# The last output tile of a gated two-branch mixer, divided at column 448 in place of 384

## The chip, the cores and the metric

The kernel runs on one core of a Trainium2 chip. The time is device time in microseconds (us). All runs quoted here are "fast" (an undisturbed clock; the profiles have a granted TensorE clock of 0.998 or 1.0). A profile is one execution; its span is about 1.7 us shorter than the time of the same run (204.5 against 206.2 for the kernel before).

Names used: PE is TensorE, PEld its weight loads, DVE is VectorE, ACT is ScalarE, SP is SyncE, which here only issues DMAs; a trailing q (ACTq, SPq) marks the issue of a DMA by that engine. L515 is line 515 of the kernel. PSUM is the memory in which PE's sums build up, in banks; SBUF is the on-chip memory from which DMAs store. To evict a tile is to copy it from PSUM to SBUF. A store is issued when an engine starts it, and has landed when the last of its 16 completion records has come. Its semaphore is the counter on which SP waits for that.

## The reference, cut to what matters

```python
x = A_x                                            # (1, 2048, 512)
g = _sigmoid((x * gate_w).sum(-1, keepdims=True))
a = _A_ref(x, A_wqkv, A_w_phi, A_wo)               # linear attention, ends in  o @ wo
b = _B_ref(x, B_w_in, B_w_sp, B_b_sp, B_w_out)     # gMLP, ends in (z1 * g) @ w_out
return g * a + (1 - g) * b
```

The output is made in 16 tiles of 128 rows and 512 columns. For each tile, PE accumulates both final products (attention with 4 matmuls, gMLP with 5 matmuls and a remainder) in one PSUM bank. Another engine multiplies the sum by `1 - g` (the gate's other factor is already inside) on its way to SBUF as bf16, and a DMA stores it.

## The kernel before: the parts that matter

Only the last of the 16 tiles is treated specially. Tiles 12, 13 and 14 wait for their remainder matmuls and are stored whole. Tile 15 is computed in two column pieces in two PSUM banks, so that the first piece can be evicted and stored while PE still works on the second.

```python
def ba_attn(acc, tt, start, stop, c0=0, c1=D):
    for g in range(NG):                                      # L509: 4 matmuls
        nc.tensor.matmul(acc, lhsT=oTs[tt][:, g, :], rhs=wo_t[:, g, c0:c1], ...)

def ba_spat(acc, tt, start, c0=0, c1=D):
    i = tt % 2
    for ft in range(5):                                      # L515: 5 matmuls
        nc.tensor.matmul(acc, lhsT=uTs[tt][:, i + ft, :], rhs=w_main[i][:, ft, c0:c1], ...)

def ba_store(acc, tt, c0=0, c1=D, on_dve=False, on_sp=False):
    ob = work.tile([P, c1 - c0], BF16, name=f"ob{c1 - c0}", bufs=4 if c1 - c0 == D else 1)
    dst = out2[tt * P:(tt + 1) * P, c0:c1]
    if on_dve:
        nc.vector.tensor_scalar(                             # L527
            out=ob[:, :], in0=acc, scalar1=g_inv[:, tt:tt + 1], scalar2=None, op0=ALU.mult)
        nc.sync.dma_start(out=dst, in_=ob[:, :])             # L529
    else:
        nc.scalar.activation(out=ob[:, :], in_=acc, func=AF.Copy, scale=g_inv[:, tt:tt + 1])  # L531
        (nc.sync if on_sp else nc.scalar).dma_start(out=dst, in_=ob[:, :])                    # L532

def ba_last():
    last = NT - 1
    ba_step(last - 1)
    pieces = [(acc_tile()[:, 0:384], 0, 384), (bank_tile(q_bank)[:, 0:P], 384, D)]
    for t in BA_GROUPS[-1][:-1]:
        ba_rem(accs[t][:, :], t)                             # L520, remainders of tiles 12 to 14
    for acc, c0, c1 in pieces:
        ba_rem(acc, last, True, c0, c1)                      # L520, remainder of each piece
    for n, t in enumerate(BA_GROUPS[-1][:-1]):
        ba_store(accs[t][:, :], t, on_dve=n == 1, on_sp=True)
    for n, (acc, c0, c1) in enumerate(pieces):
        ba_spat(acc, last, False, c0, c1)
        ba_attn(acc, last, False, True, c0, c1)
        ba_store(acc, last, c0, c1, on_dve=n == 1)           # piece 1: ACT and ACTq; piece 2: DVE and SPq
```

The softmax here doesn't subtract the row's maximum and nothing guards it: scores larger than these inputs give would overflow.

## Time and profile before

| | before |
|---|---|
| time, median of the first 3 runs | 206.33 us (206.13 to 206.88) |
| span of the profiled run | 204.5 us |
| PE busy | 200.8 us, 98% |
| last PE work ends | about 201.7 us |

The first part of the page of the kernel before (engine, busy us, share, instructions) says that PE is busy for almost all of the span:

```profile
PE 200.8 (98%) x1557; PEld 119.9 (59%) x1557; DVE 130.4 (64%) x283; ACT 74.8 (37%) x122; POOL 45.6 (22%) x76
```

The change acts only in the last 5.5 us. This is the end of the chain of waits of the kernel before (start us, us, what):

```profile
199.07 0.54 PE mm L520 x4
199.61 0.92 PE mm L515 x5
200.53 0.65 PE mm L509 x4
201.18 0.28 PE mm L515 x5
201.46 0.24 PE mm L509 x4
201.69 0.02 issue
201.72 0.35 DVE ob L527
```

The second and third lines are the nine matmuls of the 384-column piece; the fourth and fifth are those of the 128-column piece. The chain is followed back from the DVE eviction of the narrow piece: that is the eviction that ended last. The chain stops there and does not show which store landed last; that has to be read from the stores themselves. The timeline of the same stretch shows the two sides that run next to each other (start us, us, engine, line, operation, tile, shapes):

```profile
201.08 0.40 SPq L532 DMA_DIRECT2D out_dram<-ob  x1
201.21 0.58 ACT L531 ACTIVATE ob<-mm,g_inv 128x384 bf16<-128x384 f32 x1 [0.52 <-PE mm L509]
201.29 0.39 PE L509 MATMUL mm<-wspT,oT 128*128 128x128 bf16 x4
201.72 0.35 DVE L527 TENSOR_SCALAR ob<-mm,g_inv 128x128 bf16<-128x128 f32 x1 [1.45 <-PE mm L509]
201.82 0.34 ACTq L532 DMA_DIRECT2D out_dram<-ob  x1
202.09 0.33 SPq L529 DMA_DIRECT2D out_dram<-ob  x1
```

The DMA view of that stretch gives, for each of those two stores, size and us from issue to landing:

```profile
out_dram<-ob ACTq DMA_DIRECT2D x1, 96.0 KB, 1.7
out_dram<-ob SPq DMA_DIRECT2D x1, 32.0 KB, 1.6
```

So the wide piece lands near 201.82 + 1.7 = 203.5 and the narrow one near 202.09 + 1.6 = 203.7.

### The profile page before, as it was taken

Reading aid. Unit: us, or ns where it says so; the run is one execution under the profiler, and the core shown is the slowest. Engines: PE = TensorE matmul, PEld = TensorE weight load, DVE = VectorE, ACT = ScalarE, POOL = GpSimd, SP = SyncE. Lnnn points to the kernel's source line nnn. Section 1 sums busy time; section 2 is a strip of 40 time slices with the busy share of each in tenths; the row PEclk is TensorE's granted clock in tenths of the full one; section 3 lists DMA queues with packets and bytes.
Section 4 is the critical chain, followed back from the end, with each engine's and each line's share of the span. In section 5 each row is a group of like instructions: output and inputs, shape, how many; then the busy total and the mean of one; then the engine's idle time right before and its main releaser. Section 6 shows DMA issues by size and latency. Waiting matters only on the chain.

```text
span 204.5 us, 3996 instructions
## 1 busy us (share of the span) xinstructions
PE 200.8 (98%) x1557; PEld 119.9 (59%) x1557; DVE 130.4 (64%) x283; ACT 74.8 (37%) x122; POOL 45.6 (22%) x76
## 2 busy tenths in 40 slices
PE   8999999999999999999999999999999999999994
PEld 4666666655665555656565666555555555665642
DVE  4567484837977587979797789555566645633332
ACT  3566678796222333332424042222251136002303
POOL 3020202021523325334242442222204220200000
PEclk9999999999999999999999999999999999999999
DMA  6999699999999027940423219853567458552833
GB/s 194 252 205 171 80 151 290 146 278 247 256 249 213 3 38 182 287 94 16 75 48 45 51 38 120 154 109 64 105 161 80 90 113 183 63 96 51 156 64 104
DMA packets 89931, 27.22 MB, mean 133 GB/s; under 512 B 84184, under 2 KB 89912, under 8 KB 89912
## 3 DMA queue, kind: packets, MB, share of 16 engines
q1 hardware_dynamic: 87744, 24.99, 65.4%
q10 hardware_dynamic: 2168, 1.98, 3.5%
q8 instruction: 12, 0.20, 0.4%
q14 instruction: 7, 0.06, 0.1%
HBM read 4.15 MB, written 2.10 MB: 31 GB/s over the span
## 4 chain that ended last, share of the span: by engine, by line
PE 98%; DVE 0%; issue 0%
PE mm L454 37%; PE zp L191 18%; PE mm L355 14%; PE mm L515 9%; PE mm L509 7%; PE mm L395 7%; PE kvacc L411 2%; PE at L467 2%; PE zp L222 1%; PE mm L520 1%; PE zp L307 0%; PE pq L280 0%; PE at L478 0%; PE pq L307 0%; DVE ob L527 0%; PE zp L230 0%
## 5 line engine op out<-in xcount | busy, mean ns | idle before, releaser
L454 PE MATMUL mm<-z2all,wspT 128*128 128x344 bf16 x512 | 79.9, 309 | 0.0
L454 PEld LDWEIGHTS <-wspT 128*128 128x128 bf16 x512 | 49.0, 98 | 25.3
L191 PE MATMUL zp<-w_z,xT 128*128 128x344 bf16 (+1 forms) x254 | 38.1, 310 | 0.0
L359 ACT ACTIVATE eq<-mm 128x512 bf16<-128x512 f32 x32 | 17.4, 594 | 51.4 <-PE mm L355 25.7
L363 DVE TENSOR_REDUCE zs<-eq 128x64 f32<-128x1024 bf16 x16 | 19.5, 1220 | 20.0 <-ACT eq L359 20.0
L191 PEld LDWEIGHTS <-xT 128*128 128x128 bf16 x254 | 24.4, 98 | 11.8
L359 ACT ACTIVATE ek<-mm 128x512 bf16<-128x512 f32 x32 | 17.3, 600 | 27.1 <-PE mm L355 27.1
L459 DVE SCALAR_TENSOR_TENSOR ucat<-mm,bT,z1all 128x344 bf16<-128x344 f32 x32 | 17.4, 544 | 15.0 <-PE mm L454 15.0
L372 POOL TENSOR_TENSOR eq<-eq,ratio 128x512 bf16<-128x512 bf16 x16 | 16.9, 1055 | 44.6 <-DVE ratio L371 36.7
L531 ACT ACTIVATE ob<-mm,g_inv 128x512 bf16<-128x512 f32 (+1 forms) x15 | 10.1, 680 | 33.1 <-PE mm L520 28.5
L363 DVE TENSOR_REDUCE zs<-ek 128x64 f32<-128x1024 bf16 x16 | 19.3, 1209 | 2.8 <-ACT ek L359 2.8
L515 PE MATMUL mm<-wspT,uT 128*128 128x512 bf16 (+2 forms) x85 | 20.1, 367 | 0.0
L355 PEld LDWEIGHTS <-xT 128*128 128x128 bf16 x128 | 12.2, 98 | 12.0
L372 POOL TENSOR_TENSOR ek<-ek,ratio 128x512 bf16<-128x512 bf16 x16 | 16.9, 1056 | 2.2 <-DVE ratio L371 1.7
L509 PE MATMUL mm<-wspT,oT 128*128 128x512 bf16 (+2 forms) x68 | 16.6, 366 | 0.0
L355 PE MATMUL mm<-wq_p,xT 128*128 128x512 bf16 x64 | 16.4, 379 | 0.0
L395 PE MATMUL mm<-wv_sb,xT 128*128 128x512 bf16 x64 | 16.4, 379 | 0.0
L355 PE MATMUL mm<-wk_p,xT 128*128 128x512 bf16 x64 | 16.3, 379 | 0.0
L209 DVE BATCH_NORM_STATS2 bn<-z2all 128x6 f32<-128x344 bf16 x32 | 14.9, 501 | 0.0
L206 ACT ACTIVATE z2all<-zp 128x688 bf16<-128x688 f32 x16 | 11.8, 744 | 7.3 <-PE zp L191 7.2
L260 ACT ACTIVATE z1all<-zp 128x688 bf16<-128x688 f32 x16 | 11.9, 744 | 5.1 <-PE zp L191 4.6
L515 PEld LDWEIGHTS <-uT 128*128 128x128 bf16 x85 | 8.1, 98 | 9.4 <-issue 0.2
(77 smaller groups left out, 142.7 us busy)
## 6 DMA issues: line engine op xcount, KB each, us to landing
out_dram<-ob ACTq DMA_DIRECT2D x12, 128.0 KB, 2.4
wspT<-in_B_w_out_dram SPq DMA_DIRECT2D x2, 640.0 KB, 4.9
w_z<-in_B_w_in_dram SPq DMA_DIRECT2D x2, 344.0 KB, 4.7
w_z<-in_B_w_in_dram SPq DMA_DIRECT2D x3, 172.0 KB, 3.5
wv_sb<-in_A_wqkv_dram SPq DMA_DIRECT2D x2, 256.0 KB, 2.7
wspT<-in_A_wo_dram SPq DMA_DIRECT2D x2, 256.0 KB, 4.0
out_dram<-ob SPq DMA_DIRECT2D x3, 128.0 KB, 1.8
uT<-ucat SPq DMA_TRANSPOSE x16, 2.8
```

The source lines that it names most:

```text
L191: nc.tensor.matmul(zp[:, j, 0:n], lhsT=xT[:, dt, tt * P:(tt + 1) * P], rhs=wt[:, dt, j * HF:j * HF + n], start=(dt == 0), stop=(dt == NDT ...
L209: nc.vector.bn_stats(out=bn6[:, tt, j, :], in_=z2v[:, j, :])
L260: nc.scalar.activation(out=z1all[:, tt, :].rearrange("p (j n) -> p j n", j=2), in_=zp[:, :, 0:HF], func=AF.Gelu_apprx_tanh,)
L355: nc.tensor.matmul(ps[:, :], lhsT=xT[:, dt, tt * P:(tt + 1) * P], rhs=w[:, dt, :], start=(dt == 0), stop=(dt == NDT - 1))
L359: nc.scalar.activation(out=e[:, :, a, :], in_=ps[:, :].rearrange("p (h f) -> p h f", f=DH), func=AF.Exp, scale=1.0 - 2.0 * a)
L363: nc.vector.tensor_reduce(out=z[:].rearrange("p h a -> p (h a)"), in_=e[:].rearrange("p h a f -> p (h a) f"), axis=AX.X, op=ALU.add,)
L372: nc.gpsimd.tensor_tensor(out=e[:, :, 1, :], in0=e[:, :, 1, :], in1=ratio[:, :, None].to_broadcast([P, H, DH]), op=ALU.mult)
L395: nc.tensor.matmul(v_ps[:, :], lhsT=xT[:, dt, tt * P:(tt + 1) * P], rhs=wv_sb[:, dt, :], start=(dt == 0), stop=(dt == NDT - 1))
L454: nc.tensor.matmul(gp[:, 0:HF], lhsT=wspT[:, st, tt * P:(tt + 1) * P], rhs=z2all[:, st, j * HF:(j + 1) * HF], start=(st == 0), stop=(st == ...
L459: nc.vector.scalar_tensor_tensor(out=ucat[tt % NU][:, c0 + j * HF:c0 + (j + 1) * HF], in0=gp[:, 0:HF], scalar=bT[:, tt:tt + 1], in1=z1all[ ...
L509: nc.tensor.matmul(acc, lhsT=oTs[tt][:, g, :], rhs=wo_t[:, g, c0:c1], start=start and g == 0, stop=stop and g == NG - 1)
L515: nc.tensor.matmul(acc, lhsT=uTs[tt][:, i + ft, :], rhs=w_main[i][:, ft, c0:c1], start=start and ft == 0, stop=False)
```

## The change

Its intent is to make the second piece, the one that is evicted and stored after PE's last matmul, smaller, so that less work stands after the end of PE. 64 columns move from the second piece to the first.

```diff
     def ba_last():
         last = NT - 1
         ba_step(last - 1)
-        pieces = [(acc_tile()[:, 0:384], 0, 384), (bank_tile(q_bank)[:, 0:P], 384, D)]
+        cut = D - 64
+        pieces = [(acc_tile()[:, 0:cut], 0, cut), (bank_tile(q_bank)[:, 0:D - cut], cut, D)]
```

## The prediction

> **What bounds the kernel now.** PE is busy 200.8 of the 204.5 us span (98%, the page's first part), and the chain of waits is PE from start to end. The change touches only the last tile, after about 199 us. There the chain ends with five matmuls of L515 and four of L509 on 384 columns (199.61 to 201.18), the same nine on 128 columns (201.18 to 201.69), then the 128-column VectorE eviction (201.72, 0.35 us). The timeline puts the 384-column ScalarE eviction at 201.21 (0.58 us), its output DMA (ACT queue) at 201.82, and the 128-column DMA (SP queue) at 202.09. The DMA view gives 1.7 and 1.6 us to landing: about 203.5 and 203.7. The remaining 0.8 us to 204.5 is SP's closing wait and the end of the program. So two tails run side by side, and the small piece's lands last, by about 0.16 us.
>
> **What the change moves.** No arithmetic, no instruction and no byte is added or removed; 64 columns go from the second piece to the first.
>
> - First piece on PE: in the chain nine matmuls of 384 columns take 1.57 us, 0.174 each at first and 0.1625 in the steady part (0.65 us for four). 512 columns take 0.216 (1.08 us for five), so 448 should take 0.189: nine times 0.027 is +0.24 us.
> - Second piece on PE: 128 columns take 0.056 each (0.28 us for five). The matmuls of 68 columns at L467 take 0.032 each (0.26 us for eight), so 64 columns should take about 0.031, and the weight load is no floor at 0.056. Nine times 0.025 is -0.22 us. The Trainium skill ("TensorE: Matmul & The Clock Gate", Back-to-back issue gap) has N/2.4 + 2.5 ns, and about 60 cycles (25 ns) below 64 columns; the trace's 56 and 216 ns agree with the first. The last matmul thus ends about where it did, +0.00 to +0.03.
> - ScalarE eviction: 0.687 us at 512 and 0.581 at 384, so 0.634 at 448: +0.05.
> - VectorE eviction: 0.751 at 512 and 0.351 at 128, so 0.284 at 64: -0.07.
> - DMA: the first piece grows from 96 to 112 KB, perhaps +0.04 us (an estimate from about 260 GB/s in the windows of 201 to 202.5). The second shrinks from 32 to 16 KB, with as many packets of half the size: little.
>
> **What lies on the critical path.** The first piece's DMA is issued at 201.82 + 0.24 + 0.05 = 202.11 and lands near 203.84. The second's is issued at about 202.04 and lands near 203.60. The end changes hands: the wide ScalarE piece, not the narrow VectorE piece, lands last, about 0.18 us later than the end now. The two DMAs also start within 0.1 us of each other instead of 0.27 and share the engines, which may cost up to 0.2 us more. I predict 206.33 + 0.2 = 206.5 us: slightly slower, below what the 2% test sees. Range 206.15 to 207.0; the before runs alone span 206.13 to 206.88. Faster by over 2%: 0.01; within 2%: 0.98; slower: 0.01.
>
> **What the profile should show.** Everything up to 199 us unchanged; 448-column matmuls 0.189 apart; 64-column ones 0.031 apart; last PE work ending within 0.05 us of 201.69; ScalarE eviction 0.63 us, starting near 201.45; ACT-queue issue near 202.11, after the SP-queue one near 202.04; span about 204.7.
>
> **What would make it wrong.** 64-column matmuls held at the 0.056 us of the 128-column ones (+0.2 us on the second piece); the two nearly simultaneous DMA issues delaying each other; DMA rows of 128 B landing slower than those of 256 B; or a run-to-run shift larger than the effect.

## The result, and the profile after

| | before | after |
|---|---|---|
| time, median of 6 runs each | 206.31 us (205.96 to 206.88) | 206.77 us (206.37 to 207.22) |
| ratio | | 1.002, 95% interval 0.9998 to 1.0043 |
| span of the profiled run | 204.5 us | 204.7 us |

A ratio here is the mean time of one kernel's fast runs over that of the other's fast runs of the same rounds, so it is not quite the ratio of the medians. The interval includes 1: by the timed runs alone, the change could be nothing. The predicted time was 206.5 us; the measured median lies inside the predicted range, but so does 206.31, the time of no change at all. The time alone therefore does not confirm the prediction.

The traces are sharper. Here is the end of the chain of waits of the changed kernel:

```profile
199.07 0.54 PE mm L520 x4
199.61 1.05 PE mm L515 x5
200.66 0.77 PE mm L509 x4
201.43 0.02 issue
201.45 0.63 ACT ob L531
```

The chain now ends in the ACT eviction of the wide piece; the narrow piece is gone from it. In both kernels the last remainders start at 199.07 and the wide piece's matmuls at 199.61. Those took 0.92 + 0.65 = 1.57 us and take 1.05 + 0.77 = 1.82: +0.25 from these rounded figures, +0.24 costed. The timeline:

```profile
201.25 0.31 PE L515 MATMUL mm<-wspT,uT 128*128 128x64 bf16 x5
201.40 0.28 PE L509 MATMUL mm<-wspT,oT 128*128 128x64 bf16 x4
201.45 0.63 ACT L531 ACTIVATE ob<-mm,g_inv 128x448 bf16<-128x448 f32 x1 [0.77 <-PE mm L509]
201.72 0.28 DVE L527 TENSOR_SCALAR ob<-mm,g_inv 128x64 bf16<-128x64 f32 x1 [1.45 <-PE mm L509]
202.03 0.33 SPq L529 DMA_DIRECT2D out_dram<-ob  x1
202.12 0.35 ACTq L532 DMA_DIRECT2D out_dram<-ob  x1
```

The DVE eviction of the second piece starts at 201.72 in both kernels: PE ends at the same moment, because the work on it is only moved. That eviction is 0.07 us shorter and its store is issued 0.07 us earlier (0.06 from the rounded figures shown). The wide piece pays for it: eviction 0.24 us later and 0.05 us longer, store issued at 202.12 in place of 201.82. The DMA view:

```profile
out_dram<-ob ACTq DMA_DIRECT2D x1, 112.0 KB, 1.7
out_dram<-ob SPq DMA_DIRECT2D x1, 16.0 KB, 1.4
```

The wide piece now lands near 203.8 and the narrow one near 203.4. The end of the program has changed hands.

**A cleaner measure.** The start of the first L520 matmul of this last group is a good mark: nothing that the change touches comes before it. I call the time from that mark to the end of the span the *tail*, and the time before it the *head*. Landing times within the tail are the last completion record of each DMA in the trace. The tail is 204.495 - 199.000 = 5.495 us before and 204.735 - 198.999 = 5.736 us after: +0.24 us. Each tail here is that of one profiled execution; the kernel before has only one.

### The profile page after: what moved, and what is told of

Read it like the earlier page. It is cut to its first block, busy times and chain, and to the rows that moved or that the text cites. A ratio compares the mean times of both kernels' runs of the same rounds, so it can differ in the third digit from the quotient of the medians.

```text
span 204.7 us, 3996 instructions
## 1 busy us (share of the span) xinstructions
PE 200.8 (98%) x1557; PEld 119.9 (59%) x1557; DVE 130.3 (64%) x283; ACT 74.7 (36%) x122; POOL 45.6 (22%) x76
## 4 chain that ended last, share of the span: by engine, by line
PE 98%; ACT 0%; issue 0%
PE mm L454 37%; PE zp L191 18%; PE mm L355 14%; PE mm L515 8%; PE mm L395 7%; PE mm L509 7%; PE kvacc L411 2%; PE at L467 2%; PE zp L222 1%; PE mm L520 1%; PE zp L307 0%; PE pq L280 0%; ACT ob L531 0%; PE at L478 0%; PE zp L230 0%; PE pq L307 0%
```

## The experiments

Theory ("race of two tails"): the end is the later of two sides, the wide piece (PE, ACT, ACTq's DMA) and the narrow one (PE, DVE, SPq's DMA). Moving columns shifts one side against the other, and the sum of PE's work does not change. Rivals: the 1.002 is noise; the narrow DMA rows of 128 B are what costs; the two stores issued within 0.09 us of each other delay each other.

All times in this table are us after the mark. Every experiment gave a correct result.

| run | piece 1 (ACT): issued, landed | last piece (DVE): issued, landed | tail | head |
|---|---|---|---|---|
| before, cut at 384 | 2.82, 4.48 | 3.10, **4.65** | 5.50 | 199.00 |
| after, cut at 448 | 3.12, **4.83** | 3.03, 4.45 | 5.74 | 199.00 |
| `cut448_again` | 3.12, **4.82** | 3.03, 4.46 | 5.71 | 199.14 |
| `cut256b` | 2.24, 4.09 | 3.23, **4.82** | 5.65 | 199.52 |
| `cut400` | 2.90, 4.59 | 3.08, **4.79** | 5.64 | 199.28 |
| `cut416` | 2.97, 4.72 | 3.06, **4.89** | 5.74 | 199.96 |
| `cut480` | 3.26, **4.96** | 3.07, 4.74 | 5.79 | 199.03 |
| `dve2_448` | 3.12, 4.83 | 3.35, **5.05** | 5.87 | 199.61 |
| `dve2_384` | 2.83, 4.46 | 3.48, **5.29** | 6.14 | 199.39 |
| `act2_448` | 3.78, **5.47** | 3.03, 4.44 | 6.30 | 198.97 |

The landing in bold is the one that comes last. The head varies by 1.0 us between these profiles (198.97 to 199.96), four times the effect of the change; the tails of the two executions of the same changed kernel differ by 0.02. A span from a single profile, as my early expectations used it, is therefore the wrong measure, and below I read the tails.

### The change again

No edit; the changed kernel timed in five more rounds.

> The changed kernel, unedited, timed again in five rounds. Theory (race of two tails): the wide first piece's ScalarE eviction and DMA end last, 0.24 us later in the span than the narrow piece did before; ratio about 1.001, profile span 204.7. Rival (run-to-run noise made the 1.002): ratio 1.000, and the start of the closing matmuls at L520, not the tail after it, differs between runs.

Measured: 206.69 us median against 206.52 before, ratio 1.0014 (0.9996 to 1.0032). Its tail is 5.712 us (5.736 the first time), its head 0.14 us longer. The timed runs again lean to slower without excluding 1. The rival is half right: most of the scatter between profiles is in the head, yet the tail's +0.22 to +0.24 us repeats. It is 0.11 to 0.12% of the time, within both intervals.

### Other cuts: 400, 416, 480

```diff
-        cut = D - 64
+        cut = 400          # cut416: 416; cut480: 480
```

> Cut at column 400. Race theory: both tails land nearly together, wide piece near 203.60, narrow near 203.65, span 204.5, as before; no gain above 0.02 us. Rival (any narrower second piece costs, through narrow DMA rows of 224 B): span 204.55 or more.

> Cut at column 480. Race theory: the wide piece lands 0.15 us later than at 448 (nine matmuls of 32 more columns +0.12, eviction +0.03), span 204.9, and 32-column matmuls are 0.025 us apart or more. Rival (two DMAs issued within 0.1 us of each other delay one another; here they are 0.25 us apart again): span 204.7 or less.

> Cut at column 416. Race theory: the wide piece is issued 2.97 us after the first closing matmul of L520 and lands at 4.64, the narrow one is issued at 3.06 and lands between 4.55 and 4.75; tail from that matmul to the end of the span 5.48 to 5.60, where the kernel before has 5.495 and the changed one 5.736. Rival (the 400 cut was slow, 5.638, only because its rows of 800 and 224 B begin and end off a 64 B step; 832 and 192 B do not): 5.45 or less.

Measured: cut400 206.21 us against 206.52, ratio 0.9996 (0.9977 to 1.0014); cut416 206.62 against 206.15, ratio 1.0022 (1.0002 to 1.0042); cut480 206.79 against 206.52, ratio 1.002 (0.9998 to 1.0042). The tails are 5.64, 5.74 and 5.79.

cut480 follows the theory. The wide piece lands 0.13 us later than at 448 (0.15 expected), and the rival is out for that piece: the two issues are 0.19 us apart and its store took 1.69 us, against 1.71 at 448. One assumption of the theory fails here: PE ends 0.07 us later (2.75 us after the mark in place of 2.68), since the 32-column matmuls are 0.025 us apart and the 64-column ones 0.029, which saves less than the wider ones cost. The tail grew by only 0.05 us; the section on the closing waits says why.

cut400 and cut416 were misses. The issues fell where I had put them (2.90 and 3.08; 2.97 and 3.06), and the wide piece landed as expected at 400 (1.69 us after issue) and 0.08 us late at 416. But the narrow piece took 1.72 and 1.83 us from issue to landing, where it took 1.55 in the kernel before. cut400's tail is what its rival said (a narrower second piece costs); but at 448 the second piece is narrower still, its rows are 128 B, and it landed after 1.43 us. The timeline of cut416, and below it its DMA view:

```profile
202.93 0.37 ACTq L532 DMA_DIRECT2D out_dram<-ob  x1
203.03 0.33 SPq L529 DMA_DIRECT2D out_dram<-ob  x1
```

```profile
out_dram<-ob ACTq DMA_DIRECT2D x1, 104.0 KB, 1.8
out_dram<-ob SPq DMA_DIRECT2D x1, 24.0 KB, 1.8
```

The two stores are issued 0.09 us apart, ACT's first, and both take 1.8 us. With the same distance and SP's first (the changed kernel) the narrow store takes 1.4. The two differ in width too (96 and 64 columns), so the comparison at one width counts for more: the same 64-column store took 1.43 us issued before ACT's (after) and 1.70 issued 0.23 us behind it (dve2_448, below). The packet records say where it begins: from SP's issue to its first data packet are 0.83 us when SP's is first (after), 0.99 when it follows ACT's by 0.09 (cut416), 0.96 by 0.18 (cut400), 0.96 by 0.23 (dve2_448), 0.86 by 0.27 (before), and 0.83 when ACT's issue is 0.66 us old (dve2_384). That is 0.17 of the 0.40 us between after and cut416; the rest comes behind the first packet, about half of it while the data moves, in part beside the packets of ACT's store, and half between the last data packet and the landing. All 16 reports of the store come late in cut416 (the first 1.65 us after issue, against 1.25), so it is not the single late share that is described further down. So the prediction's warning about nearly simultaneous issues was right for the order ACT, SP and wrong for the order SP, ACT, which is the one that the change produced. The rival about rows off a 64 B step falls: cut416 is on that step and is not faster than cut400. I can show the dependence on order and distance, not what in the DMA path makes it; a cut at 416 with SP's store issued first was not run.

### Cut at 256, and a mistake of mine

```diff
-        cut = D - 64
+        cut = 256
```

> Cut at column 256. Race theory: the second piece, now 256 columns, ends last: its VectorE eviction takes 0.485 us in place of 0.351 and its DMA grows, span 204.65 to 204.75. Rival (narrow rows make the second piece slow, wider ones are better): span below 204.5.

Measured: 207.74 us against 206.52, ratio 1.0068 (1.0045 to 1.0092). That is far more than the 0.15 to 0.25 us expected, and the trace shows an error in the experiment:

```profile
202.98 0.48 DVE L527 TENSOR_SCALAR ob<-mm,g_inv 128x256 bf16<-128x256 f32 x1 [2.94 <-DMA out_dram<-ob]
203.49 0.33 SPq L529 DMA_DIRECT2D out_dram<-ob  x1
```

The DVE eviction waited for a DMA and not for PE. The tile name is made from the width (`ob256`), with one buffer; two pieces of equal width share it, so the second had to wait until the first was stored. The mended trial names the buffer by its column too:

```diff
-        ob = work.tile([P, c1 - c0], BF16, name=f"ob{c1 - c0}", bufs=...)
+        ob = work.tile([P, c1 - c0], BF16, name=f"ob{c1 - c0}_{c0}", bufs=...)
```

> Cut at column 256 with a separate output buffer for each piece; in the first trial both pieces had the same tile name and one buffer, so the second eviction waited for the first piece's output DMA. Race theory: second eviction starts 2.72 us after the first closing matmul of L520, takes 0.485, issued 3.23, landing 1.5 to 1.6 later, tail 5.58 to 5.70. Rival (wide second pieces are better): below 5.45.

Measured: 206.58 us against 206.15, ratio 1.0017 (0.9993 to 1.0041); tail 5.65. The second eviction starts 2.72 after the mark, the store is issued at 3.23 and lands 1.59 later, all as expected. The wider rows (512 B) did not make the store land sooner (1.59 us against 1.55 before), though it also carries twice the bytes. So the tail is longer on both sides of 384, and 384 has the shortest tail of the six widths tried, each but 448 profiled once. The timed runs do not resolve this (cut400 has a ratio of 0.9996), and cuts between 256 and 384 were not tried.

### Which side is critical

```diff
-            nc.vector.tensor_scalar(
-                out=ob[:, :], in0=acc, scalar1=g_inv[:, tt:tt + 1], scalar2=None, op0=ALU.mult)
+            for _ in range(1 if c1 - c0 == D else 2):        # dve2_448 and dve2_384
+                nc.vector.tensor_scalar(
+                    out=ob[:, :], in0=acc, scalar1=g_inv[:, tt:tt + 1], scalar2=None, op0=ALU.mult)
```

dve2_384 makes this edit to the kernel before, dve2_448 to the changed one. act2_448 does the same to the ACT eviction of the changed kernel. The same values are written twice, so the result stays right.

> Changed kernel, the wide piece's ScalarE eviction done twice. Race theory: this piece ends last, so all of about 0.55 us more shows: span 205.3. Rival (the narrow piece ends last): the first 0.2 us or more are hidden, span 205.0 or less.

> Kernel before, the narrow piece's VectorE eviction done twice. Race theory: this piece ends last, so all of the 0.3 us more shows: span 204.8. Rival (something else ends last): span stays 204.5.

> Changed kernel, the narrow piece's VectorE eviction done twice (same values written twice). Race theory: that piece has about 0.4 us of slack, so its 0.25 us more do not show: span 204.7 to 204.8. Rival (the narrow piece still ends last, because of its 128 B rows): span 205.0.

Measured medians: act2_448 206.89, dve2_384 206.92, dve2_448 206.72, against 206.74 before in the same rounds; ratios 1.0012, 1.0008 and 1.0005, all intervals containing 1. The tails decide. The ends of the timelines of act2_448, dve2_384 and dve2_448, in this order:

```profile
201.42 1.30 ACT L532 ACTIVATE ob<-mm,g_inv 128x448 bf16<-128x448 f32 x2 [0.76 <-PE mm L509]
202.00 0.33 SPq L529 DMA_DIRECT2D out_dram<-ob  x1
202.75 0.34 ACTq L533 DMA_DIRECT2D out_dram<-ob  x1
```

```profile
202.10 0.74 DVE L528 TENSOR_SCALAR ob<-mm,g_inv 128x128 bf16<-128x128 f32 x2 [1.45 <-PE mm L509]
202.21 0.34 ACTq L533 DMA_DIRECT2D out_dram<-ob  x1
202.87 0.33 SPq L530 DMA_DIRECT2D out_dram<-ob  x1
```

```profile
202.33 0.60 DVE L528 TENSOR_SCALAR ob<-mm,g_inv 128x64 bf16<-128x64 f32 x2 [1.45 <-PE mm L509]
202.73 0.34 ACTq L533 DMA_DIRECT2D out_dram<-ob  x1
202.96 0.33 SPq L530 DMA_DIRECT2D out_dram<-ob  x1
```

Read against the kernel that each one edits:

- act2_448: the store is issued 0.67 us later than in the changed kernel, lands 0.65 later, and the tail is +0.57 (0.55 expected). The wide piece is critical after the change. The two stores are 0.76 us apart in this run and took 1.41 us (narrow) and 1.69 (wide); 0.09 apart, in the changed kernel, 1.43 and 1.71. So the rival that two near issues delay each other is worth some 0.02 us in this order, SP first.
- dve2_384: issued 0.39 us later than in the kernel before, landed 0.65 later, tail +0.65 (0.3 expected). The narrow piece is critical before the change. The extra 0.26 us goes with a stray packet, discussed below; the late share was this store's own, and without it the store would still have landed last (15 of its 16 reports by 4.93, the wide piece at 4.46), so the reading stands.
- dve2_448: issued 0.32 us later than in the changed kernel, landed 0.59 later; tail only +0.14. Most of the delay was slack, as the theory says, but the expected +0.06 or less was exceeded: the narrow store was now issued 0.23 us after ACT's and took 1.70 us in place of 1.43, so it landed last by 0.2. The 0.37 us of slack in the changed kernel could not all be used: once SP issued second, its store took longer.

### The order of the closing waits

```diff
             ba_attn(acc, last, False, True, c0, c1)
-            ba_store(acc, last, c0, c1, on_dve=n == 1)
+        for n, (acc, c0, c1) in reversed(list(enumerate(pieces))):
+            ba_store(acc, last, c0, c1, on_dve=n == 1)
```

> Changed kernel, the two last stores written in the opposite order in the program; each engine's own work stays the same. Only the semaphores of the two output DMAs trade places in SP's closing waits. Theory: of the 0.24 us by which the span grew, 0.06 us is the second closing wait, standing after the wait that releases last; with the order turned the span is 204.67 or 204.68. Rival (all 0.24 us is landing time): span stays 204.73.

Measured: 206.82 against 206.74, ratio 1.0006 (0.9981 to 1.0032); tail 5.713. This run decided nothing about the waits: the semaphores did not trade places, the trace shows the same order. It does serve as a third trial of the changed kernel (tail +0.22). Other runs answer the question. In cut480 and act2_448 the semaphore of ACT's last store happens to be waited for last, and the span ends 0.83 us after the last landing (5.787 - 4.958, 6.302 - 5.473). In the changed kernel and its repeat that store also lands last but is waited for next to last: 5.736 - 4.825 = 0.91 and 5.712 - 4.821 = 0.89. Before, where the narrow store lands last and is waited for last, it is 0.85. So 0.04 to 0.08 us of the change's 0.24 are one more wait after the landing, which the prediction had not counted; in the trace of the changed kernel SP's last two waits end 0.06 us apart. It is also why the tail of cut480 is only 0.05 longer than that of 448.

### Can the division beat 384 at all?

Three pieces of 256, 192 and 64 columns, so that the ACT piece is narrow and early:

```diff
-        cut = D - 64
-        pieces = [(acc_tile()[:, 0:cut], 0, cut), (bank_tile(q_bank)[:, 0:D - cut], cut, D)]
+        cuts = (0, 256, 448, D)
+        banks = (acc_tile(), bank_tile(q_bank), bank_tile(g_bank))
+        pieces = [(t[:, 0:c1 - c0], c0, c1) for t, c0, c1 in zip(banks, cuts, cuts[1:])]
...
-            ba_store(acc, last, c0, c1, on_dve=n == 1)
+            ba_store(acc, last, c0, c1, on_dve=n != 1)
```

> Three pieces of 256, 192 and 64 columns, evicted by VectorE, ScalarE and VectorE. Race theory: the piece evicted by ScalarE is only 192 columns wide, is issued near 201.90 and lands near 203.5; the 64-column piece is issued near 202.05 and lands near 203.5; span 204.3, some 0.15 us below the kernel before, ratio 0.999. Rival (the count of DMAs or of narrow rows costs): span 204.5 or more.

Measured: 206.99 us (206.89 to 209.41) against 206.32, ratio 1.0045 (1.0005 to 1.0084); tail 6.10. Slower, against the theory; one run of 209.41 makes up about half of the ratio's excess, but the median is 0.67 us higher too. The issues are where they should be, but the DMA view of the trace shows three slow stores (some lines left out):

```profile
q14 instruction: 1, 0.01, 1.2%
issues: line engine op xcount, KB each, median us to landing
out_dram<-ob SPq DMA_DIRECT2D x1, 128.0 KB, 1.8
out_dram<-ob SPq DMA_DIRECT2D x1, 64.0 KB, 2.2
out_dram<-ob ACTq DMA_DIRECT2D x1, 48.0 KB, 2.0
out_dram<-ob SPq DMA_DIRECT2D x1, 16.0 KB, 2.1
```

Each store is spread over 16 DMA engines and reports from each. Of the 64-column store's 16 reports, 15 had come by 4.65 us after the mark and the last came at 5.14. The first line above is a DMA of the instruction queue: one packet of 8 KB, starting 3.47 after the mark and taking 0.70 us. If it sits on one of the 16 engines, it explains one late share in each store; the trace does not name the engine. The Trainium skill ("Runtime: NRT & Kernel Launch", Instruction fetch mechanics) says that each sequencer fetches its next page of instructions by its own DMA queue while it executes; ("DMA: Bandwidth & Descriptors", Issuing engines are not separate DMA queues) that DMAs begun by the scalar, sync or gpsimd engine all run on the same 16 DMA engines and interleave. That section does not speak of instruction fetches; that this packet shares an engine with the stores is my reading. In the ten profiles whose ACT instructions in the trace number 195 this packet starts 1.30 to 1.48 us after ACT's last output store is issued, wherever that store stands. With 196 it starts 0.54 us after it in `three` and 0.34 in cut480; with 197, in act2_448, 2.25 us before it. That points to ACT's program, and gives a test: make it two instructions longer, far from the tail.

```diff
-    nc.scalar.activation(
-        out=scrap[:, :], in_=nc.const_aps.tensor(1.0, [P, 1], BF16), func=AF.Gelu_apprx_tanh)
+    for _ in range(3):
+        nc.scalar.activation(
+            out=scrap[:, :], in_=nc.const_aps.tensor(1.0, [P, 1], BF16), func=AF.Gelu_apprx_tanh)
```

> The three pieces, with two more one-column activations at the start of ScalarE's program, in its idle time before 4.5 us. In the trial without them one 8 KB packet of the instruction queue held one DMA engine for 0.70 us just when the three output DMAs needed it, and the last of 16 shares of each landed 0.5 us after the other 15. Theory: that packet belongs to ScalarE's instruction stream and comes earlier with more ScalarE instructions (0.5 to 3 us earlier); then it misses the output DMAs, the last landing is at about 4.65 in place of 5.143, and the tail is about 5.5 in place of 6.097, no better than the kernel before (5.495). Rival (three output DMAs are slow by themselves): tail still 6.0 or more.

Measured: 206.6 us against 206.15, ratio 1.0016 (0.9995 to 1.0037); tail 5.59. The packet now comes 1.44 after the mark, 2.0 us earlier, and the DMA view of the same stretch has no instruction packet left:

```profile
out_dram<-ob SPq DMA_DIRECT2D x1, 128.0 KB, 1.8
out_dram<-ob SPq DMA_DIRECT2D x1, 64.0 KB, 1.6
out_dram<-ob ACTq DMA_DIRECT2D x1, 48.0 KB, 1.6
out_dram<-ob SPq DMA_DIRECT2D x1, 16.0 KB, 1.6
```

The last landing is at 4.64 (4.65 expected). So the packet's place follows the length of ACT's program, and the slow stores go with the packet; the test was run once. The same late share is in dve2_384: 15 of 16 reports by 4.93, the last at 5.29, with the packet running from 4.13 to 4.67. It is in cut480's narrow store too: 15 by 4.48, the last at 4.74, with the packet from 3.60 to 4.05; there it cost nothing, as the wide piece landed later.

Without the accident three pieces still do not win: the last landing equals that of the kernel before (4.64 against 4.65), and from there to the end it is 0.95 us in place of 0.85, with more closing waits. None of the divisions tried has a shorter tail than the cut at 384.

## Why the prediction was right

- **What bounds the end.** Right. Before, the narrow piece lands last, by 0.16 us (4.646 - 4.482). dve2_384 showed it: delay on that side came through in full.
- **PE's work is only moved.** Right. Nine 448-column matmuls are 0.189 us apart and nine 64-column ones 0.029 (0.031 predicted); PE ends 2.678 us after the mark in both kernels. The weight load is no floor at 0.056: the 128-column matmuls are that far apart, the 64-column ones half that.
- **Evictions.** Right: 0.633 us (0.634 predicted) on ACT, 0.283 (0.284) on DVE.
- **The end changes hands.** Right. ACT's store is issued at 202.12 (202.11 predicted) and lands at 203.82 (203.84); act2_448 showed that this side is critical. The larger store took 0.05 us longer to land (1.66 to 1.71 us). The predicted +0.04 is close, though its own basis, 16 KB at 260 GB/s, gives 0.06.
- **The narrow store** landed about 0.15 us earlier than predicted (203.45 against 203.60), which goes with its being issued ahead of ACT's (dve2_448: 1.70 us behind it, 1.43 ahead). That cost nothing, as it had slack.
- **The term missed.** "About 0.18 us later than the end now" was +0.24 in the trace. The landings moved by 0.18 (4.825 - 4.646), as predicted; the other 0.06 is SP's second closing wait, which stood before the last landing and now stands behind it. The possible 0.2 us for two stores issued close together did not occur in this order; a delay of that kind does occur in the other (cut416, dve2_448).
- **The time.** 206.5 predicted, 206.77 and 206.69 measured in two batches, against 206.31 and 206.52 before: +0.46 and +0.17. That the number fits is in part luck, and the range was wide enough to hold no change as well. The tails are worth +0.22 to +0.24; the rest is taken to be scatter of the head, which is larger than that. Comparing the times of the same VectorE instructions in the traces, the slowest of them is already behind early and stays so: cut416 against before is +1.08 us at the eighth microsecond and +0.96 at the 182nd.

## What to carry to other kernels

Splitting the last tile buys overlap only until the second side catches the first: when two evictions and two stores run next to each other, find which lands last before making the other one smaller, since work taken from one side is added to the other. For effects far below the run-to-run scatter, measure from a mark just ahead of the change to the end of the program within the trace, and use the timed runs only to confirm that nothing larger happened. When one store is slow for no visible reason, look at its shares: where one of 16 was late here, a single other packet stood in the same stretch; where all 16 were late, it went with the order of the issues.

## What the Trainium skill lacked or had wrong

- "TensorE: Matmul & The Clock Gate", Back-to-back issue gap: it gives about 81 ns per matmul at 128 columns and about 131 ns at 512 for streams of weight load and matmul pairs. This case's streams of such pairs run at 56 ns and 216 ns, which is its formula for the isolated gap (N/2.4 + 2.5 ns). Its table puts 1 to 64 columns together at about 60 cycles (25 ns; the prediction says "below 64", but the row includes 64); measured are 29 ns at 64 columns (the formula) and 25 ns at 32 (the table).
- "DMA: Bandwidth & Descriptors", Specifications: it warns of read-modify-write below 512 B. The packet records of these stores show no step there: the median packet took 11 ns at 64 B, 13 at 128, 18 at 256, 27 at 512 and 47 at 1024. Narrow rows do move fewer bytes per ns, as the page's warning has it, but in the changed kernel that hardly counted: all data packets of the store with 128 B rows lie within 0.23 of its 1.43 us.
- The same page, Issuing engines are not separate DMA queues: it does not say that the order of two nearly simultaneous issues matters. A 64-column SP store issued 0.09 us before ACT's landed after 1.43 us; issued 0.23 us after it, 1.70 us (dve2_448). A 96-column one issued 0.09 us after it took 1.83 us (cut416).
- "Runtime: NRT & Kernel Launch", Instruction fetch mechanics: it speaks of 16 KiB refills whose cost is mostly hidden. One instruction queue of this trace has packets of 16 KB; the packet at the end, of another queue, is 8 KB and takes 0.34 to 0.71 us. Where it met the last stores, their last share landed 0.26 us (cut480) to 0.60 us (three) after the other 15.
- No page mentions that the order of the closing waits counts: 0.83 to 0.85 us from the last landing to the end of the program where it is waited for last, 0.89 to 0.91 where one more wait follows, 0.95 where two do (three, three_shift).
